# An issue order read from a table instead of planned at build time, in a fused attention and two-MLP kernel on one core

## The chip, the cores and the metric

The kernel runs on one core of a Trainium2 chip. A core has five engines with an instruction queue each: PE (TensorE, the matmuls), DVE (VectorE), ACT (ScalarE), POOL (GpSimd) and SP (SyncE, which here issues every transfer). The engines run side by side and wait for each other through semaphores. The metric is the device time of one execution in microseconds, lower is better.

## The reference, cut to what matters

```python
# attention with decay, 2 batches x 8 heads, 768 positions, 64 wide, in blocks of 64
for b in range(nb):
    intra = einsum('bhic,bhjc->bhij', qb, kb) * Dmask
    intra = einsum('bhij,bhjd->bhid', intra, vb)
    inter = einsum('bhid,bhde->bhie', qb * lam_pow, kv_state)
    out[:, :, sl] = intra + inter
    kv_state = lam_block * kv_state + einsum('bhsd,bhse->bhde', kb * rev_pow, vb)
x = out as 1536 tokens x 512
x = (sigmoid(x @ w_gate) * (x @ w_val)) @ w_out      # 512 -> 1536 -> 512
h = x @ w_in
return elu(h) @ w_out2                               # 512 -> 2048 -> 512
```

All inputs are float32.

## The kernel before, in words

The attention goes over six chunks of 128 positions. For each chunk `scores` multiplies keys with queries (tile `st`, from `tin`) and updates the running state (`st<-nat,kd`), and the loop multiplies the masked scores with the values (`x<-pr,nat`) and the queries with the state (`x<-ql,sn`); `split_chunk` then turns the result into the operands of the MLPs. These attention matmuls are plain float32 and use parts of PE's array (64 or 128 rows, 64 columns); the trace shows them as 64\*64 and 128\*64. The MLPs run in the format of 32 bits rounded for PE (the trace's fp32r), on the whole array, 128\*128: each number is split into a high and a low part, and each product takes three matmuls. They go over hidden columns in groups of 256 (six in the first MLP, eight in the second) and use Strassen-Winograd products of half-size blocks, so that DVE, ACT and POOL have many additions between. Weights come in pieces of 1 MB through one buffer `w64`, are rebuilt into floats in `w32` by `fetch` (one ACT and two DVE instructions for each), and are then summed and split. Results gather in `acc`, and the output leaves in 13 transfers from `o`.

`A0`, `B0` and so on are PSUM banks: the trace names a bank's tile after its first use, so that `warm` in the trace is any tile in bank A0 and `direct` any in B0. In the first microseconds 18 matmuls on a zeroed tile `idle` keep PE running while the first loads land (line 771).

Nothing is issued where it is written. Every call in the body is recorded by `Work.record` (line 167) as an `Op` with an estimated duration; `hazards` (line 207) finds what each operation must stay behind; `issue` (line 408) then makes up the order and emits all operations in it. Within an engine the emitted order is the order of execution. The order before comes from a planner: `run` (line 271) is a list scheduler on a model of the five engines, run forwards and backwards for several settings of `stick` (how long PE keeps to one kind of matmul, since a change of kind costs it time) and of `ahead`; `exchange` (line 385) puts the best stages of several plans together, with the borders set by `mark`. The costs are those of `cost` (line 140): for a transfer 440 ns of the queue, and its bytes at 423 bytes a nanosecond.

Below, operations go by the number that `record` gives them, and PE's operations also by their place in PE's order. One operation of the attention stands for a block of 16 to 32 matmuls.

Of the kernel before, what the change touches and what calls it, by code (L numbers as in the profile page):

```python
# [19 lines left out]
P = 128  # L20
B, H, S, D = 2, 8, 768, 64
# [15 lines left out]
WORDS = 4096  # L37

# [89 lines left out]
class Work:  # L128
# [6 lines left out]
    def __init__(self, nc):  # L135
        self.nc, self.ops, self.block, self.marks = nc, [], None, [0]
        for name in ENGINES:
            setattr(self, name, Engine(self, name))

    def cost(self, op, fn, args, kw):  # L140
# [13 lines left out]
        if fn == "dma_start":  # L154
            return 440, n * P * 4 / 423 if op.eng == "sync" else 2000
# [115 lines left out]
    def run(self, preds, key, backward=False, gate=None, stick=0, thrift=20000):  # L271
        ops = self.ops[::-1] if backward else self.ops
        n = len(ops)
        after, left = [[] for _ in range(n)], [len(p) for p in preds]
        for k, p in enumerate(preds):
            for x in p:
                after[x].append(k)
        ripe, soon = {e: [] for e in ENGINES}, {e: [] for e in ENGINES}
        at, start, end = [max(0.0, g) for g in gate] if gate else [0.0] * n, [0.0] * n, [0.0] * n
        free = dict.fromkeys(ENGINES, 0.0)  # L280
        port = behind = 0.0
        queue = 3500.0
        shape = table = None
        told, pages = 0, {}

        def stall(op, t, keep=False):
            late = 0.0
            here = {}
            for m in range((told + self.FIRST) // self.PAGE, (told + op.words + self.FIRST + self.LEAD) // self.PAGE + 1):
                for mark in (m * self.PAGE - self.FIRST - self.LEAD, m * self.PAGE - self.FIRST):  # L290
                    if m < 2 or not told <= mark < told + op.words:
                        continue
                    now = t + late + op.gap * (mark - told) / op.words
                    if mark == m * self.PAGE - self.FIRST:
                        late += max(0.0, here.get(m, pages.get(m, 0)) - now)
                    else:
                        here[m] = now + (self.SLOW if queue > now + 2000 else self.FAST)
            if keep:
                pages.update(here)
            return late  # L300

        for k in range(n):
            if not left[k]:
                heapq.heappush(soon[ops[k].eng], (at[k], k))
        for _ in range(sum(op.eng is not None for op in ops)):
            t, e = min((free[e] if ripe[e] else max(free[e], soon[e][0][0]), i, e)
                       for i, e in enumerate(ENGINES) if ripe[e] or soon[e])[::2]
            while soon[e] and soon[e][0][0] <= t:
                k = heapq.heappop(soon[e])[1]
                heapq.heappush(ripe[e], (key[k], k))  # L310
            rank, k = heapq.heappop(ripe[e])
            if e == "tensor" and stick and ops[k].shape != shape:
                like = min((x for x in ripe[e] if x[0] < rank + stick and ops[x[1]].shape == shape), default=None)
                if like:
                    ripe[e].remove(like)
                    heapq.heapify(ripe[e])
                    heapq.heappush(ripe[e], (rank, k))
                    k = like[1]
            if e == "tensor" and not backward and thrift and stall(ops[k], t) > 100:
                like = min((x for x in ripe[e] if x[0] < rank + thrift and not stall(ops[x[1]], t)), default=None,  # L320
                           key=lambda x: (ops[x[1]].words, x))
                if like:
                    ripe[e].remove(like)
                    heapq.heapify(ripe[e])
                    heapq.heappush(ripe[e], (rank, k))
                    k = like[1]
            op = ops[k]
            if e == "sync":
                late = 300 if queue < t + 2000 or t < 3000 else 1100
                queue = max(t + 2000, queue) + op.took  # L330
                free[e], end[k] = t + op.gap, queue + late
            elif e == "tensor":
                t += 60 if t > free[e] + 1 else 0
                t += self.SWITCH if op.shape != shape else 0
                shape = op.shape
                late = 0.0
                if not backward:
                    late = stall(op, t, True)
                    told += op.words
                free[e], end[k] = t + late + op.gap, t + late + op.took  # L340
            else:
                if op.table and op.table != table:
                    t, table = t + self.TABLE, op.table
                go = max(t, port, behind if e == "gpsimd" else 0) if op.port else t
                free[e], end[k] = go + op.gap, go + op.took
                if op.port:
                    port = free[e]
                    behind = end[k] + self.HANDOFF["gpsimd"] if e == "vector" else 0
            start[k] = t
            done = [k]  # L350
            while done:
                x = done.pop()
                for s in after[x]:
                    f = ops[s].eng
                    near = e == "tensor" or e == "sync" and (ops[s].prev is op or op.prev is ops[s])
                    ready = free[e] if f == e and x == k and near else end[x] + self.HANDOFF.get(f, 0)
                    at[s] = max(at[s], ready)
                    left[s] -= 1
                    if left[s]:
                        continue  # L360
                    if f is None:
                        start[s] = end[s] = at[s]
                        done.append(s)
                    else:
                        heapq.heappush(soon[f], (at[s], s))
        return start, end

    def mark(self):
        self.marks.append(len(self.ops))

    def clocks(self, plans):
        work = [sum(op.gap for op in self.ops[:m] if op.eng == "tensor") for m in self.marks[1:]]
        clocks = []
        for start, end in plans:
            order = sorted((start[k], op.gap) for k, op in enumerate(self.ops) if op.eng == "tensor")
            at, done, clock = 0, 0.0, [0.0]
            for w in work:
                while done + order[at][1] <= w:
                    done += order[at][1]
                    at += 1  # L380
                clock.append(order[at][0] + w - done)
            clocks.append(clock + [max(end)])
        return clocks

    def exchange(self, preds, plans, tries=8):
        bounds = self.marks + [len(self.ops)]
        best = min(plans, key=lambda x: max(x[1]))
        for i in list(range(len(self.marks))) * 2:
            clocks = self.clocks(plans)
            mine = self.clocks([best])[0]  # L390
            ranked = sorted(range(len(plans)), key=lambda r: clocks[r][i + 1] - clocks[r][i])
            for r in ranked[:tries]:
                gain = mine[i + 1] - mine[i] - clocks[r][i + 1] + clocks[r][i]
                if gain <= 0:
                    break
                key = list(best[0])
                for k in range(bounds[i], bounds[i + 1]):
                    key[k] = plans[r][0][k] - clocks[r][i] + mine[i]
                for k in range(bounds[i + 1], len(self.ops)):
                    key[k] -= gain  # L400
                made = self.run(preds, key)
                plans.append(made)
                if max(made[1]) < max(best[1]):
                    best = made
                    mine = self.clocks([best])[0]
        return best

    def issue(self, tc, rounds=7):
        self.hazards()
        n = len(self.ops)  # L410
        preds = [op.preds for op in self.ops]
        turned = [[] for _ in range(n)]
        for k, p in enumerate(preds):
            for x in p:
                turned[n - 1 - x].append(n - 1 - k)
# [33 lines left out]
def tile_decay_attention_two_mlps(  # L449
# [314 lines left out]
    n = 1  # L764
# [309 lines left out]
    for i in range(1, NG1):  # L1074
# [3 lines left out]
        if i in (2, NG1 - 1):  # L1078
            work.mark()
# [118 lines left out]
```

## Time and profile before

| | us |
|---|---|
| median of 3 runs | 582.1 |
| lowest and highest | 581.39, 582.28 |
| the profiled execution | 581.52 |
| its span, first to last instruction | 579.6 |
| PE busy in the span | 569.1 |
| DVE, ACT, POOL busy | 447.8, 312.6, 317.2 |

The profiled execution took 581.52 us, 1.9 us more than the span that its trace covers, and 0.6 us less than the median. A sum that is made on the span is carried over to the median as a difference. PE is busy for nearly the whole span, and a busy PE is not one at its peak: its matmuls overlap, so what counts is the time from the start of one to the start of the next. The attention takes the first 70 us or so, the first MLP runs to about 320 us, and the second to the end; the weight of one group of columns is in use while the next one is prepared.

### The profile page before, as it was taken

How to read it: one execution, taken by the hardware profiler on the slowest of the kernel's cores; microseconds unless marked ns; L12 is line 12 of the kernel's file. 1: busy time of each engine (PE TensorE's matmuls, PEld its weight loads, DVE VectorE, ACT ScalarE, POOL GpSimd, SP SyncE). 2: the span in 40 equal slices, each digit the busy share in tenths (PEclk: the TensorE clock that was granted, in tenths of full speed). 3: DMA queues.
4: the chain of work that ended last, by engine and by line, in shares of the span. 5: the costliest groups of instructions: out<-in, count | busy, mean ns of one | idle time of the engine just before them, and what ended most of it. 6: DMA issues, size and time to landing. Idle time of an engine off the chain costs nothing.

```text
span 579.6 us, 10208 instructions
## 1 busy us (share of the span) xinstructions
PE 569.1 (98%) x3998; PEld 487.2 (84%) x3998; DVE 447.8 (77%) x771; ACT 312.6 (54%) x612; POOL 317.2 (55%) x273
## 2 busy tenths in 40 slices
PE   7899999999999999999999999999999999999997
PEld 4788898888888888888898888888888888888886
DVE  6877844679999989989978994777676667686484
ACT  4893656445345345444457887764746554735160
POOL 2677678875365555553688865574738180712100
PEclk9999999999999999999999999999999999999999
DMA  8946211221221211210140222232222222200014
GB/s 298 411 168 219 75 74 74 74 74 72 74 73 67 80 47 73 98 55 21 72 146 2 74 73 74 72 144 76 73 74 72 74 74 73 74 0 1 0 37 181
DMA packets 10271, 52.03 MB, mean 90 GB/s; under 512 B 1264, under 2 KB 1520, under 8 KB 5744
## 3 DMA queue, kind: packets, MB, share of 16 engines
q1 hardware_dynamic: 10224, 51.39, 24.4%
q8 instruction: 31, 0.51, 0.3%
q14 instruction: 16, 0.13, 0.1%
HBM read 48.24 MB, written 3.15 MB: 89 GB/s over the span
## 4 chain that ended last, share of the span: by engine, by line
PE 89%; ACT 4%; DVE 3%; DMA 3%; issue 1%; SPq 0%; POOL 0%; ACTq 0%; DVEq 0%
PE xu L182 35%; PE st L182 32%; PE direct L182 10%; PE warm L182 9%; PE x L182 2%; DMA w<-in_w_val 1%; DMA w<-in_w_gate 1%; ACT kd L182 1%; ACT w L182 1%; DVE sig L182 1%; DVE sums L182 1%; DVE gl L182 0%; DVE xu L182 0%; ACT sig L182 0%; ACT x143h L182 0%
## 5 line engine op out<-in xcount | busy, mean ns | idle before, releaser
L182 DVE TENSOR_TENSOR acc<-xu,acc 128x512 f32<-128x512 f32 x144 | 96.8, 684 | 21.7 <-PE xu L182 20.9
L182 POOL TENSOR_TENSOR t<-w 128x256 f32<-128x256 f32 (+1 forms) x80 | 69.3, 887 | 70.2 <-DVE w L182 57.6
L182 PE MATMUL xu<-gl,woh 128*128 128x512 f32 (+1 forms) x274 | 107.2, 391 | 0.1
L182 PE MATMUL xu<-gh,woh 128*128 128x512 f32 (+1 forms) x274 | 106.9, 394 | 0.3 <-DVE xt L182 0.2
L182 PE MATMUL xu<-gh,wol 128*128 128x512 f32 (+1 forms) x274 | 106.5, 389 | 0.0
L182 POOL TENSOR_TENSOR wol<-w,woh 128x512 fp32r<-128x512 f32 x34 | 43.4, 1294 | 67.2 <-ACT woh L182 66.5
L182 POOL TENSOR_TENSOR gl<-sig,gh 128x512 fp32r<-128x512 f32 (+1 forms) x30 | 55.0, 1844 | 40.0 <-ACT gh L182 23.9
L182 POOL TENSOR_TENSOR l<-t,h 128x768 fp32r<-128x768 f32 (+1 forms) x38 | 62.6, 1654 | 13.0 <-ACT h L182 4.9
L182 ACT CAST gh<-sig 128x512 fp32r<-128x512 f32 (+1 forms) x66 | 46.7, 714 | 32.5 <-DVE sig L182 31.6
L182 PEld LDWEIGHTS xu<-gh,woh 128*128 128x128 f32 x274 | 51.4, 188 | 11.3 <-DVE xt L182 0.8
L182 PEld LDWEIGHTS xu<-gh,wol 128*128 128x128 f32 x274 | 51.5, 188 | 10.4
L182 PEld LDWEIGHTS xu<-gl,woh 128*128 128x128 f32 x274 | 51.5, 188 | 10.0 <-DVE gl L182 0.5
L182 ACT ACTIVATE sig<-st 128x512 f32<-128x512 f32 (+1 forms) x52 | 29.2, 566 | 53.4 <-PE st L182 35.5
L182 DVE SCALAR_TENSOR_TENSOR w<-w,w 128x1024 uint32<-128x1024 uint32 (+1 forms) x36 | 54.0, 1503 | 0.3
L182 PE MATMUL st<-x143l,h 128*128 128x512 f32 (+1 forms) x150 | 51.8, 347 | 0.0
L182 PE MATMUL st<-x143h,h 128*128 128x512 f32 (+1 forms) x150 | 51.3, 347 | 0.0
L182 PE MATMUL st<-x143h,l 128*128 128x512 f32 (+1 forms) x150 | 50.7, 347 | 0.0
L182 ACT ACTIVATE w<-w 128x1024 f32<-128x1024 f32 (+1 forms) x36 | 39.3, 1092 | 18.0 <-POOL l L182 10.5
L182 DVE TENSOR_SCALAR w<-w 128x1024 uint32<-128x1024 uint32 (+1 forms) x36 | 32.2, 896 | 18.8 <-ACT w L182 18.6
L182 DVE TENSOR_TENSOR wt<-st,wt 128x512 f32<-128x512 f32 (+1 forms) x57 | 31.5, 556 | 14.2 <-PE st L182 13.9
L182 ACT CAST h<-t 128x768 fp32r<-128x768 f32 (+1 forms) x40 | 29.1, 727 | 13.0 <-POOL t L182 12.8
L182 ACT ACTIVATE sig<-sig 128x256 f32<-128x256 f32 (+1 forms) x68 | 34.2, 510 | 1.3
(190 smaller groups left out, 1495.3 us busy)
## 6 DMA issues: line engine op xcount, KB each, us to landing
w<-in_w_out SPq DMA_DIRECT2D x14, 1024.0 KB, 4.8
w<-in_w_in SPq DMA_DIRECT2D x8, 1024.0 KB, 4.8
nat<-in_att SPq DMA_DIRECT2D x12, 512.0 KB, 9.9
w<-in_w_gate SPq DMA_DIRECT2D x5, 1024.0 KB, 4.8
w<-in_w_val SPq DMA_DIRECT2D x5, 1024.0 KB, 4.8
tin<-in_att SPq DMA_DIRECT2D x6, 512.0 KB, 9.7
tin<-in_att SPq DMA_DIRECT2D x3, 1024.0 KB, 11.4
out_t<-o SPq DMA_DIRECT2D x11, 256.0 KB, 2.0
```

Source lines behind the costliest of these rows:

```text
L182: return [getattr(getattr(self.nc, eng), fn)(*(real(a) for a in args), **{k: real(a) for k, a in kw.items()})]
```

## The change

The planner is taken out (`run`, `mark`, `clocks`, `exchange` and the loop in `issue`), and with it the import of `heapq` and the two calls of `work.mark()`. In its place stands a text constant, `ORDER_TABLE`. `order` decompresses it into one 16-bit step for each recorded operation, sums the steps up to a place for each operation, checks that there are as many places as operations and that no operation stands ahead of one it must follow, and returns the operations in order of place. The emission of the order is the same as before, with the dependencies that it adds between DVE and POOL. The body of the kernel, the tiles, the arithmetic and the transfers are untouched. In `cost` the transfer's two numbers are changed; with the planner gone no order is made from them in the kernel.

```diff
+ORDER_TABLE = (
+    'c-qZa35;FUdH(;i-h0m7-Zsmd@yvL}V{DI&?GcXI8uplqr79_<5+F5Ag<7>y*Qg|IBBG|MKr~$_L`qfBAgZ(h7a=7!1Q)P_19pf_yayZa#>;'
...
+)
...
         if fn == "dma_start":
-            return 440, n * P * 4 / 423 if op.eng == "sync" else 2000
+            return 500, n * P * 4 / 410 if op.eng == "sync" else 2000
...
-    def run(self, preds, key, backward=False, gate=None, stick=0, thrift=20000):
...
-    def issue(self, tc, rounds=7):
+    def order(self):
+        raw = np.frombuffer(zlib.decompress(base64.b85decode("".join(ORDER_TABLE))), np.uint8)
+        steps = np.ascontiguousarray(raw.reshape(2, -1).T).view("<i2")[:, 0].astype(int)
+        places = np.cumsum(steps) + np.arange(len(steps))
+        assert len(places) == len(self.ops), "the table is of another program"
+        assert all(places[p] < places[k] for k, op in enumerate(self.ops) for p in op.preds), "an order against a hazard"
+        return np.argsort(places).tolist()
+
+    def issue(self, tc):
         self.hazards()
-        n = len(self.ops)
...
-        start, end = self.exchange(preds, plans)
-        best = max(end), start
-        order = sorted(range(n), key=lambda k: (best[1][k], k))
+        order = self.order()
         behind = mybir.DependencyInfo(mybir.DependencyClass.Sync, mybir.DependencyReason.DATA)
```

The table can be read without running anything: decompressed, it gives the new order of each engine. Some of both orders, as operation numbers:

| | before | new |
|---|---|---|
| operations of PE, DVE, ACT, POOL, SP | 2961, 771, 609, 269, 71 | the same |
| at the same place in the engine's order | | 153, 82, 67, 66, 71 |
| PE, places 24 to 60 | 135, 2 MLP matmuls, 141, 8, 136, 6, 142, 8, then 160, 161, 286, 162, 163, 287, 292, 165, 228 | 135, 141, 21 MLP matmuls, 142, 136, 3, then 160 to 162, 286, 287, 163, 292, 165, 293 |
| ACT, places 13 to 25 | 74, 76, 62 to 65, 78, 66, 80, 67, 68, 69, 214 | 76, 74, 80, 63, 78, 210, 66, 68, 65, 67, 62, 69, 64 |
| ACT, places of 134 (first sigmoid), 166, 168 | 37, 47, 48 | 47, 49, 51 |
| PE's last 12 places | 4665 to 4670, 4673 to 4678 | the same |

135 and 141 are `st<-tin` of chunk 1, 136 and 142 its `st<-nat,kd`, 286 and 292 `st<-tin` of chunk 2, 287 and 293 its `st<-nat,kd`, 160 to 163 and 165 the `x` of chunk 1, 62 to 69 and 150 to 157 the `kd` of chunks 0 and 1 (ACT), 74, 76 and 166, 168 the casts `x11h` of chunks 0 and 1 (ACT), 210 the cast `h25` of a sum that POOL makes, and 228 on the products of chunk 0 with the first values' weight.

## Rows read from the trace of the kernel before

**Rows 1.** The page: span, busy time by engine, PE and its clock in 40 slices

```profile
span 579.6 us, 10208 instructions
PE 569.1 (98%) x3998; PEld 487.2 (84%) x3998; DVE 447.8 (77%) x771; ACT 312.6 (54%) x612; POOL 317.2 (55%) x273
...
PE   7899999999999999999999999999999999999997
...
PEclk9999999999999999999999999999999999999999
```

**Rows 2.** PE's waits for transfers: engine, tile, releaser: us in total, times, longest us

```profile
PE st L182 <- DMA tin<-in_att: 1.4, 2, 0.9
```

**Rows 3.** Timeline of PE to 23 us: start us, busy us, instruction, [idle before]

```profile
11.74 1.78 PE L182 MATMUL x<-pr,nat 64*64 64x64 f32 x64 [2.13 <-DVE w L182]
...
22.86 0.90 PE L182 MATMUL st<-tin 64*64 64x128 f32 x32 [0.89 <-DMA tin<-in_att]
```

**Rows 4.** Windows of 10 us: busy us (instructions) of PE, PEld, DVE, ACT, POOL

```profile
20.00:30.00 10.00, 8.94 (x206) 8.08 (x207) 9.71 (x17) 9.97 (x29) 7.01 (x6) 1.00 1.03 412
...
170.00:180.00 10.00, 10.00 (x53) 8.59 (x52) 9.93 (x15) 4.25 (x8) 8.05 (x8) 1.00 0.30 107
```

**Rows 5.** Timeline of ACT from 15 to 28 us

```profile
15.72 1.28 ACT L182 ACTIVATE kd<-nat,low 128x128 f32<-128x128 f32 x4 [1.20 <-DMA nat<-in_att]
...
23.54 1.28 ACT L182 ACT_TABLE_LOAD   x1
...
27.82 1.05 ACT L182 CAST x11h<-x 128x512 fp32r<-128x512 f32 x2
```

**Rows 6.** Timeline of PE where its kind of matmul changes

```profile
23.69 1.15 PE L182 MATMUL x<-pr,nat 128*64 128x64 f32 x32
24.67 0.64 PE L182 MATMUL st<-nat,kd 128*64 128x64 f32 x16
...
36.82 0.64 PE L182 MATMUL x<-pr,nat 128*64 128x64 f32 x16
37.38 0.39 PE L182 MATMUL warm<-x11h,l 128*128 128x256 f32 x1
37.61 0.40 PE L182 MATMUL direct<-x11h,h 128*128 128x256 f32 x2
...
51.95 0.28 PE L182 MATMUL direct<-x22l,h 128*128 128x256 f32 x1
52.07 0.28 PE L182 MATMUL direct<-x22h,l 128*128 128x256 f32 x1
52.28 0.69 PE L182 MATMUL st<-nat,kd 128*64 128x64 f32 x16
```

**Rows 7.** Timeline of PE, its larger stops from 23 to 80 us

```profile
28.44 0.51 PE L182 MATMUL direct<-x11h,h 128*128 128x256 f32 x2 [0.17 <-ACT x11h L182]
...
35.17 1.20 PE L182 MATMUL x<-pr,nat 64*64 64x64 f32 x32 [0.41 <-ACT kd L182]
...
71.66 0.35 PE L182 MATMUL warm<-x11h,h 128*128 128x256 f32 x1 [0.50 <-ACT xPh L182]
```

**Rows 8.** Timeline of PE around a short stop in the MLPs

```profile
276.24 0.28 PE L182 MATMUL st<-xPh,l 128*128 128x256 f32 x1
276.49 0.50 PE L182 MATMUL xu<-gh,woh 128*128 128x512 f32 x1
276.82 0.40 PE L182 MATMUL xu<-gl,woh 128*128 128x512 f32 x1
```

**Rows 9.** Timeline of the last microseconds: a result handed over, and its bank used again

```profile
574.56 0.28 PE L182 MATMUL xu<-gh,woh 128*128 128x256 f32 x1
...
574.76 1.14 DVE L182 TENSOR_TENSOR o<-xu,acc 128x512 f32<-128x512 f32 x2 [0.67 <-PE xu L182]
...
575.51 0.39 PE L182 MATMUL xu<-gh,woh 128*128 128x256 f32 x1
```

More of the change, by code (lines that the diff above doesn't have):

```diff
@@ L1 @@
-import heapq
+import base64
 import re
+import zlib
 from contextlib import ExitStack, contextmanager
@@ L135, in __init__ @@
     def __init__(self, nc):
-        self.nc, self.ops, self.block, self.marks = nc, [], None, [0]
+        self.nc, self.ops, self.block = nc, [], None
         for name in ENGINES:
@@ L269, in hazards @@
             op.preds = sorted(before)
-    def run(self, preds, key, backward=False, gate=None, stick=0, thrift=20000):
[L272 to L406, printed above, removed]
@@ L408, in issue @@
-    def issue(self, tc, rounds=7):
-        self.hazards()
-        n = len(self.ops)
[L411 to L415, printed above, removed]
-        best, plans = None, []
-        for stick in (0, 1500, 4000, 10000, 20000):
-            for ahead in (8e3, 20e3):
-                key, gate, least = list(range(n)), None, 1e9
-                for _ in range(rounds):
-                    start, end = self.run(preds, key, gate=gate, stick=stick)
-                    least = min(least, max(end))
-                    plans.append((start, end))
-                    if best is None or max(end) < best[0]:
-                        best = (max(end), start)
-                    _, back = self.run(turned, [-end[n - 1 - k] for k in range(n)], True)
-                    key = [-back[n - 1 - k] for k in range(n)]
-                    gate = ahead and [least + k - ahead for k in key]
-        start, end = self.exchange(preds, plans)
-        best = max(end), start
-        order = sorted(range(n), key=lambda k: (best[1][k], k))
+    def order(self):
[5 more added lines that the diff above has]
+        return np.argsort(places).tolist()
@@ L1077, in tile_decay_attention_two_mlps @@
         last = i + 1 == NG1
-        if i in (2, NG1 - 1):
-            work.mark()
         wG = prep_pair(w_gate, i, nc.gpsimd)
@@ L1111, in tile_decay_attention_two_mlps @@
         last = i + 1 == NG2
-        if i in (2, NG2 - 1):
-            work.mark()
         wH = prep_pair(w_in2, i, nc.gpsimd)
```

46 lines of the change are left out of this document (added).

## The prediction

> **What bounds the kernel now.** I read the page first: the span is 579.6 us and PE is busy 569.1 of them, at full speed of its clock, with thin slices only at the two ends [rows 1]. DVE, at 77%, comes next, and in the middle of the first MLP it is busy 9.93 of 10 us, yet PE runs there without a gap [rows 4]. So the kernel is bound by PE, and the order can change only what PE loses between its matmuls. The work itself stays: the same 3,998 matmuls.
>
> The losses are of three kinds. (1) The start. The first `x` starts only at 11.74 us, when its values have landed, and PE stops again at 22.86 us for the keys and queries of chunk 2, still in flight [rows 3]; twice and 1.4 us together it waits for such a tile [rows 2]. DMA is saturated then: 412 GB/s in the window from 20 us [rows 4]. (2) Changes of kind in the attention. From one 256-column matmul to the next there are 0.12 us (51.95 to 52.07), but 0.21 when an attention block follows (52.07 to 52.28): 0.09 lost. The first MLP matmul behind a block takes 0.23 (37.38 to 37.61) where 0.12 would do: 0.11 lost. And the block of 16 ahead of it takes 0.56 (36.82 to 37.38), where two blocks in a row take 0.98 (23.69 to 24.67), 0.49 each: 0.07 lost [rows 6]. A round trip costs 0.27 us. (3) Stops, where PE waits for another engine. The larger ones before 80 us stand in [rows 7]. Behind 80 us I went through all starts of matmuls against their usual spacing (0.227 us for 512 columns, 0.12 for 256): some 25 stops, 5.4 us together, most of them between 268 and 353 us. One of them shows the price: at 276.24 the next start comes after 0.25 instead of 0.12 us, and the matmul behind the stop takes 0.33 instead of 0.227, so a wait of 0.13 us costs 0.23 [rows 8].
>
> **The change, part by part.** The table decoded is the change; no time comes out of it, only orders. I set them against the order of the trace.
>
> *Transfers.* SP's order is the same in all 71 places, so a load starts earlier or later only where the instruction that frees its buffer moves. The transfer numbers in `cost` are read by no planner any more: 0 us. For the weights of the MLPs nothing was to be had from later landings: PE's only waits with a transfer as their releaser are the two for `tin` [rows 2]. Up to 22.86 us nothing can be gained: the loads in front are the same ten in the same order.
>
> *Up to 22.86 us.* The new order puts one more block of `x` (0.5 us) ahead of operation 286, so less is left when the load lands. But its `kd` come later on ACT: the cast 210 now stands between them, and the last `kd` of chunk 0 is ACT's 26th operation, not the 25th. In the trace the `kd` start at 15.72 [rows 5], and eight of them with two copies end at about 18.7; with the cast (0.7 us) that is 19.4. PE, which now runs 21 matmuls first, comes to 142 at about 18.0, waits for 19.4, and then the masked scores (four DVE instructions of 0.5 us, three of them ahead of the second `x`) hold the `x` until 21.9 and 22.4; 286 starts near 23.3. Half a microsecond less to do, half a microsecond later: 0, between -0.5 and +0.5.
>
> *Changes of kind behind 22.86 us.* Of 40 in the old order the new one keeps 30: four round trips between attention and MLP matmuls fewer (8 entries instead of 12), and two changes between attention shapes. Four times 0.27 are 1.1 us; for the two others, which no row shows alone, I take between 0 and 0.1 each, nearest to the exit's 0.07. Together -1.2 us (-0.8 to -1.4). Nothing can hide this: PE is the bound there.
>
> *ACT from 23 to 31 us.* ACT is busy 9.97 of 10 us in that window [rows 4], so what it does first decides. The new order puts the casts 210 and 87 (0.7 us each) and the second half's `kd` ahead, and the table load with the first sigmoid (1.28 us and 0.5, at 23.54 in the trace [rows 5]) from place 37 to 47, directly ahead of the casts `x11h` of chunk 1. The first of these began at 27.82; item by item I get about 29.1. PE needs them at its places 73 and 75 and has enough other work for all but 0.3 to 0.8 us. +0.5 us (0 to +1.0).
>
> *The stops from 28 to 80 us.* The old order's stops at 28.44, 35.17 and 71.66 [rows 7] cost, counted from start to start with the slow matmul behind them, 0.4, 0.5 and 0.8 us: 1.7. Counted in PE's own work between what they wait for and themselves, the first two get more room, by 1.0 and 2.1 us. The third falls to two matmuls (565 and 558): one gets 2.6 us more room, the other 0.4 less. The first two gained and half of the third are 1.3 us (0 to -1.7).
>
> *The stops behind 80 us.* For each of some 2,650 PE operations I took the chain from the last matmul that it hangs on, through the other engines by their mean durations, and the PE work that the order puts between; the difference is its spare time. The shortest chain is a result taken out of a bank and the bank used again: at the end of the trace a slot ends at 574.56, DVE starts at 574.76, and PE starts at 575.51, 0.95 us in all, where the order had six matmuls (0.72 us) between; it stopped for 0.23 [rows 9]. In the old order 11 operations have under 0.2 us to spare and 65 under 0.5; in the new one 79 and 166. Of the 65, three stopped, for 0.12 to 0.26 us. At that rate 166 give eight, five more, at 0.13 us and up, with 0.1 behind each [rows 8]: about +1.2. Against it, the stops of the old order with long chains (at 311 to 317 us and later) mostly get more room in the new one; I take half a microsecond for that. +0.6 us, between -3 (over half of the 5.4 us gone) and +4.
>
> *The end.* The last 12 matmuls are the same; one matmul of the group before (4654) stands three places later, so its result is handed over 0.7 us later. The stop of 0.23 us [rows 9] changes its place, not its size: 0 (-0.1 to +0.2).
>
> The sum: 0 - 1.2 + 0.5 - 1.3 + 0.6 + 0 = -1.4 us on a span of 579.6, 578.2. The profiled execution took 1.9 us more than its span, and 0.6 less than the median, so the median comes to 582.1 - 1.4 = 580.7 us.
>
> One page speaks for much more room. The Trainium skill, "Perfetto Trace Analysis", section "Identifying the Most-Contended Engine", says that PE's distance to its limit is read from the busy share of the weight loads, not from that of the matmuls. By the 84% here [rows 1] as much as 16% of the span would be open to an order. The spacing of the matmuls, which is at its floor but for the stops counted above, doesn't bear that out, and I give it no chance.
>
> **The rivals.**
>
> *A much better order*: over half of the stops behind 80 us vanish as well, and the time falls by 3.5 us or more, to about 577.5. For it speaks that most old stops get more room; against it, the thinner spare times.
>
> *Gains eaten up*: the changes of kind bring their 1.2 us, and new stops of the same size take them, so that the time stays within 1.2 us of before, say 581.9. That is the case, too, in which the table is just another order of the same worth. For it speaks that the sum is small beside its unknowns.
>
> *Slower by thin spare times.* The place is the MLPs behind 80 us, the mechanism is a bank that is handed back late because DVE, at 9.93 of 10 us, is still at something else [rows 4], the price 0.23 us each [rows 8]. Eleven more stops, one in seven of the 79 thin places, cost 2.5 us, which is more than the 1.2 of the changes of kind; thirteen and no gain at the stops before 80 us give 582.1 + 3.0 - 1.2 + 0.5 = 584.4. From about six extra stops on, the change is no gain. Against it: in the old order none of the nine places with 0 to 0.2 us to spare stopped.
>
> *Slower by ACT's queue in the attention*: the casts of chunk 1 come late for every chunk that follows, and the loads that wait for the freed buffers with them. At 15.72 ACT stood for 1.20 us at a `kd` whose transfer had not landed, with the copies of a finished `x` behind it [rows 5]. This rests on ACT working in order. The Trainium skill, "TensorE: Matmul & The Clock Gate", in its table of the engine's data, says the same: a strict queue on ACT, DVE and POOL, and on PE only weight loads pulled forward. A late item of 1 us in each of three chunks less the 1.2 us and half of the gained stops gives +1.1 us, near 583.3.
>
> **How the numbers follow.** A measurement of this kernel can tell a change of about 0.2%, 1.2 us, from none. A moderate gain, the forecast: 0.37. The much better order: 0.08. Together faster: 0.45. Gains eaten up: 0.31. Thin spare times: 0.17, ACT's queue: 0.07, together slower: 0.24. The bounds of all parts added up would reach from 572 to 588, which would need all of them to err to one side; the range from 577.3 to 584.4 leaves out about 1 in 10 on either side. It takes in the much better order's time and that of the thin spare times; the forecast's own range is 578.6 to 580.9.
>
> **What would show it.** Right: `st<-tin` of chunk 2 starts between 22.8 and 23.4 us; 30 changes of kind behind it; no stop at 35 us; PE reaches the first MLP's second group about 1 to 2 us earlier; a handful more stops of 0.1 to 0.3 us in the MLPs, at accumulations (`xu`) above all. Wrong: a stop of over 0.5 us before 45 us, for `x11h` or `kd`; stops behind 80 us of over 8 us together, or under 3; a load landing later than before.

## The result and the profile after

| | before | after |
|---|---|---|
| median, us | 582.0 | 585.5 |
| lowest and highest, us | 581.39, 582.28 | 584.42, 586.22 |
| the profiled execution, us | 581.52 | 584.42 |
| its span, us | 579.6 | 582.3 |

The change made the kernel slower: the ratio of the times is 1.0059, with a 95% interval from 1.0044 to 1.0074, or 3.5 us. (Five executions of each; the median of before came out as 581.98.) The profiled execution of the new kernel is the lowest of its five, so the traces show 2.7 us of the difference; what the rest is made of no trace shows.

The page after, span, busy time by engine, PE and its clock in 40 slices, against [rows 1]:

```profile
span 582.3 us, 10146 instructions
PE 571.6 (98%) x3998; PEld 483.7 (83%) x3998; DVE 434.5 (75%) x771; ACT 314.4 (54%) x612; POOL 313.5 (54%) x273
...
PE   7799999999999999999999999999999999999997
...
PEclk9999999999999999999999999999999999999999
```

PE is busy 2.5 us longer for the same 3,998 matmuls at the same clock, and the page says no more than that. Where the time goes is found by setting the start of each matmul against the start of the one that has the same amount of PE's own work ahead of it in the other trace (times between two starts are interpolated):

| PE's own work done, us | at, before | at, after | difference |
|---|---|---|---|
| 14 | 21.22 | 21.09 | -0.13 |
| 17 | 25.22 | 24.89 | -0.33 |
| 20 | 28.62 | 29.21 | +0.60 |
| 35 | 44.55 | 44.83 | +0.29 |
| 62 | 73.64 | 72.11 | -1.53 |
| 68 | 80.19 | 78.20 | -1.99 |
| 80 | 92.32 | 90.64 | -1.68 |
| 150 | 162.65 | 162.72 | +0.06 |
| 300 | 314.98 | 316.68 | +1.70 |
| 450 | 468.21 | 469.80 | +1.59 |
| 556.7 (just ahead of the last matmul) | 576.14 | 578.89 | +2.75 |

At 80 us the new order leads by 2.0 us, as forecast. From there to the end it loses 4.7 us, in small pieces. The view of waits, for PE's matmuls from 92 to 576 us (tile, releaser: us in total, times, longest us), first before, then after, hardly shows them:

```profile
PE xu L182 <- DVE xt L182: 0.2, 1, 0.2
```

```profile
PE direct L232 <- DVE wt L232: 0.2, 1, 0.2
PE warm L232 <- ACT wt L232: 0.2, 1, 0.2
PE st L232 <- POOL l L232: 0.2, 1, 0.2
```

The same view of the weight loads (PEld) does. Before, the four largest of 12 lines, which come to 5.7 us in 21 waits:

```profile
PEld st L182 <- DVE sig L182: 1.3, 5, 0.4
PEld xu L182 <- DVE xt L182: 0.8, 2, 0.4
PEld xu L182 <- DVE acc L182: 0.7, 3, 0.3
PEld xu L182 <- DVE gl L182: 0.5, 1, 0.5
```

After, the six largest of 16, which come to 10.7 us in 45 waits:

```profile
PEld xu L232 <- DVE acc L232: 2.0, 11, 0.2
PEld st L232 <- DVE sig L232: 1.8, 8, 0.3
PEld st L232 <- POOL l L232: 1.3, 4, 0.6
PEld direct L232 <- DVE wt L232: 1.1, 3, 0.4
PEld xu L232 <- ACT gh L232: 0.9, 4, 0.3
PEld warm L232 <- ACT wt L232: 0.8, 3, 0.4
```

A weight load stands ahead of its matmul, and it is the load that waits for the matmul's operand. It can be late without its own matmul being late; the matmul behind pays. One such place of the kernel after, PE's matmuls (start, busy):

```profile
161.36 0.28 PE L232 MATMUL warm<-xPl,h 128*128 128x256 f32 x1
161.48 0.50 PE L232 MATMUL xu<-sums,woh 128*128 128x512 f32 x1
161.82 0.40 PE L232 MATMUL xu<-xt,woh 128*128 128x512 f32 x1
162.05 0.39 PE L232 MATMUL xu<-sums,woh 128*128 128x512 f32 x1
```

then their weight loads, and DVE, which frees the bank:

```profile
161.25 0.19 PEld L232 LDWEIGHTS warm<-xPl,h 128*128 128x128 f32 x1
161.47 0.19 PEld L232 LDWEIGHTS xu<-sums,woh 128*128 128x128 f32 x1
161.58 0.19 PEld L232 LDWEIGHTS xu<-xt,woh 128*128 128x128 f32 x1
161.82 0.19 PEld L232 LDWEIGHTS xu<-sums,woh 128*128 128x128 f32 x1
```

```profile
160.74 0.68 DVE L232 TENSOR_TENSOR acc<-xu,acc 128x512 f32<-128x512 f32 x1
```

DVE is done at 161.42 (160.74 + 0.68). The matmul at 161.48 starts on time, 0.12 behind the one before, and no idle time is marked. But its load began only at 161.47, the next load at 161.58, and the next matmul comes 0.34 instead of 0.227 us later. Below, such a place is called a near miss: the operand is there 0.06 to 0.15 us ahead of the matmul that reads it.

Counted behind 92 us over all starts of PE, with a matmul as "waiting" if the last instruction that it depends on ended less than 0.062 us before its start (worked out from the starts and ends in the traces; no view shows it):

| | before | after |
|---|---|---|
| matmuls that wait | 18 | 22 |
| near misses | 19 | 56 |
| lost at the waits and directly behind them, us | 4.31 | 4.25 |
| lost directly behind near misses, us | 0.92 | 3.08 |
| changes from 256 to 512 columns | 139 | 343 |
| lost in steps of up to 0.02 us each, us | 1.89 | 4.22 |
| together, us | 7.1 | 11.5 |

The loss of 4.4 us behind 92 us is 2.2 behind near misses and 2.3 in steps of up to 0.02 us; the waits cost the same in both. The experiments had to find what both come from.

### The profile page after: what moved, and what is told of

It is laid out like the page before. It is cut to its first block, busy times and chain, and to the rows that moved or that the text cites. A ratio compares the mean times of both kernels' runs of the same rounds, so it can differ in the third digit from the quotient of the medians.

```text
span 582.3 us, 10146 instructions
## 1 busy us (share of the span) xinstructions
PE 571.6 (98%) x3998; PEld 483.7 (83%) x3998; DVE 434.5 (75%) x771; ACT 314.4 (54%) x612; POOL 313.5 (54%) x273
## 4 chain that ended last, share of the span: by engine, by line
PE 91%; ACT 3%; DMA 3%; issue 1%; DVE 1%; POOL 0%; SPq 0%; DVEq 0%; ACTq 0%
PE xu L232 37%; PE st L232 33%; PE direct L232 10%; PE warm L232 9%; PE x L232 2%; ACT kd L232 2%; DMA w<-in_w_val 1%; DMA w<-in_w_gate 1%; POOL l L232 0%; ACT w L232 0%; ACT h L232 0%; SPq L232 0%; ACT x11h L232 0%; ACT x143h L232 0%; DVE o L232 0%
## 5 line engine op out<-in xcount | busy, mean ns | idle before, releaser
L232 PE MATMUL xu<-gh,wol 128*128 128x512 f32 (+1 forms) x274 | 105.1, 391 | 0.0
L232 PE MATMUL xu<-gl,woh 128*128 128x512 f32 (+1 forms) x274 | 105.0, 391 | 0.0
L232 PE MATMUL st<-x143h,h 128*128 128x256 f32 (+1 forms) x150 | 50.5, 351 | 0.0
L232 DVE SCALAR_TENSOR_TENSOR w<-w,w 128x1024 uint32<-128x1024 uint32 (+1 forms) x36 | 45.6, 1268 | 0.4
L232 ACT ACTIVATE sig<-st 128x512 f32<-128x512 f32 (+1 forms) x52 | 29.2, 566 | 29.0 <-DVE st L232 15.8
L232 DVE TENSOR_SCALAR w<-w 128x1024 uint32<-128x1024 uint32 (+1 forms) x36 | 28.6, 797 | 13.1 <-ACT w L232 12.6
L232 ACT CAST h<-t 128x512 fp32r<-128x512 f32 (+1 forms) x40 | 29.0, 726 | 16.9 <-POOL t L232 15.8
```

The lines of the kernel that those rows point to most:

```text
L232: return [getattr(getattr(self.nc, eng), fn)(*(real(a) for a in args), **{k: real(a) for k, a in kw.items()})]
```

## Experiments

In the diffs the order is told as operation numbers of PE, since the table itself can't be read; "W us" is an amount of PE's own work. All kernels are the new one with another table, and the body is the same, unless it is said otherwise. Ratios are against the kernel before on the same chip.

### Attention or MLPs: each half with the other order

The first pair cuts at 80 us of PE's work (about 92 us).

```diff
-order = new
+order = new up to W = 80 us, then old        (e1_att_new_mlp_old)
+order = old up to W = 80 us, then new        (e2_att_old_mlp_new)
```

> The new order up to PE's work that the old order has done at 92 us, the old order for all behind it. Theory A (the new order gains in the attention and loses in the MLPs): about 1.7 us under the kernel before, 580.3 (579.5 to 581.0). Theory B (ACT's queue in the attention makes the loss): 584 or more. Nothing is left out of the computation.

> The opposite: the old order to the same point, the new one behind it. Theory A: the MLPs' loss without the attention's gain, 582.0 + 4.5 = 586.5 (585.5 to 587.5). Theory B: 582 (581.5 to 582.7).

Measured: 586.6 us (ratio 1.0075 [1.0057, 1.0094]) and 589.5 us (1.0121 [1.0104, 1.0138]). The first lies where theory B has it (584 or more), the second where neither does. But the totals can't decide here: the two orders have different matmuls behind them at the cut, and the seam makes stops of its own; the first kernel's PE, and its clock in windows of 4 us (the columns are busy us and instructions of PE, PEld, DVE, ACT, POOL, then the granted clock, DMA share, GB/s):

```profile
120.14 0.80 PE L226 MATMUL st<-x11h,h 128*128 128x512 f32 x1 [2.30 <-ACT sig L226]
```

```profile
116.00:120.00 4.00, 1.84 (x14) 1.56 (x12) 3.97 (x6) 0.51 (x1) 3.25 (x3) 1.00 0.00 0
120.00:124.00 4.00, 3.86 (x17) 3.55 (x18) 2.37 (x7) 1.67 (x4) 2.52 (x2) 0.57 0.01 2
```

The totals say nothing, then, but the course behind the seams does: from the work that the kernel before does at 126 us to the end, the kernel with the old MLPs loses 0.2 us against it, the one with the new MLPs 3.0, and the change itself 3.2. So the loss goes with the order in the MLPs.

The cut was then put where only 14 operations of all engines lie on different sides, at 60 us of PE's work (about 71 us).

```diff
-order = new
+order = new up to W = 60 us, then old        (e6_seam70_new_old)
+order = old up to W = 60 us, then new        (e7_seam70_old_new)
```

> The new order up to about 71 us (60 us of PE's own work), where only 14 operations of all engines lie on different sides in the two orders, and the old order behind it. In the traces the new order was 0.6 us ahead there. Theory A (the attention came out as forecast, the loss is made in the MLPs): 582.0 goes to 581.4 (580.8 to 581.9). Theory C (the new attention leaves later work late, ACT's queue above all, and the MLPs pay for it): 584 or more.

> The other way round: the old order up to about 71 us, the new one behind it. Theory A (the loss is made in the MLPs): 585.5 + 0.6 = 586.1 (585.4 to 586.8). Theory C (the loss comes from the new attention): 582.0 to 582.6.

Measured: 583.0 (1.0012 [0.9994, 1.0030]) and 586.6 us (1.0079 [1.0063, 1.0095]). The second agrees with theory A: the old attention in front of the new MLPs is as slow as the change. The first lies between the theories, and its executions spread as those of no other kernel, from 581.1 to 586.9, five of twelve at or below 581.8, where theory A has them. The profiled one, 586.9, shows what comes on top in some:

```profile
59.48 0.44 PE L225 MATMUL x<-ql,sn 64*64 64x128 f32 x5 [2.20 <-issue]
```

```profile
56.00:60.00 4.00, 1.80 (x43) 1.32 (x40) 2.50 (x5) 1.65 (x3) 1.71 (x2) 1.00 0.14 55
60.00:64.00 4.00, 4.00 (x22) 4.00 (x23) 2.64 (x8) 1.88 (x7) 2.52 (x2) 0.57 0.02 4
```

PE stands for 2.20 us at no wait that the profile shows, and behind it the granted clock is 0.57 on average, part of the 4 us at the lower of its two levels. The new attention has this stop in other kernels too, at the same block of matmuls (2.03 us in the first hybrid), while the trace of the change has none there.

What PE waits for can be read from the traces. They hold 16 stops of over 0.2 us that the profile calls "issue", in the twelve traces of the whole kernel, and these stand at two places only, whatever the order: behind 223 of PE's matmuls (in eleven traces, near 17 us) and behind 1,113 (in five, near 58 us), or one less where a record is missing. Each of the 16 ends 1.29 to 1.56 us behind the end of a transfer on the instruction queue (q8 in the profile): behind the first such transfer at the one place, behind the eighth at the other. In e6 the eighth falls in the window from 56.9 to 58.2 us and ends at 57.92; after the change it falls in the one from 54 to 56.9 and ends at 55.49, before PE is there:

```profile
q8 instruction: 1, 0.02, 4.4%
```

```profile
q8 instruction: 1, 0.02, 1.9%
```

So what PE waits for there is its own instructions, as far as traces can tell; no run moved these transfers alone. Why they land later in one kernel than in another is open; from 54 to 56.9 us the loads (q1) had 71.5% of the DMA engines' time in e6 and 25.0% after the change. The rest of e6's excess is 1.9 us between 300 and 400 us of PE's work, most of it one stop of 1.49 us at 368.63, behind a weight load for which ACT had waited 1.76 us.

### The widths of the matmuls

The steps of up to 0.02 us sit on 512-column matmuls behind 256-column ones, and the new order changes width more than twice as often. To see whether the widths alone cost time, the old order got 150 more changes, by exchanging two neighbours at places with at least 0.6 us to spare:

```diff
-1451 1452 1453 1535 1536 1537 1538 1539 1540 1597
+1451 1452 1535 1453 1536 1537 1538 1539 1597 1540
```

(1535 to 1540 have 256 columns, the others 512.)

> The old order, in which 150 pairs of neighbouring matmuls of PE are swapped, one of 512 and one of 256 columns each, at places with at least 0.6 us to spare on both sides; the orders of the other engines are as they were. PE then goes from 256 to 512 columns 304 times instead of 154. Theory A1 (a 512-column matmul is slower for a few places behind a 256-column one, some 14 ns for each change as the two traces have it): 150 times 14 ns, +2.1 us, 584.1 (583.2 to 585). Theory A2 (the loss in the MLPs is only late hand-overs at thin places): no change, 582.0 (581.6 to 582.5).

Measured: 583.95 us (1.0032 [1.0022, 1.0042]), as A1 said. Of the 2.1 us that the trace loses behind 92 us, 1.3 are in the steps of up to 0.02 us, 0.009 for each of 146 changes there; the rest is at five more waits. So 0.0125 us for each change, the price taken for the next expectations, was too much: it had some waits in it.

PE alone was measured with this (attention, MLPs and all else left out, the output is zeros):

```diff
+    runs("s512", [(512, 6, 0)] * 32)
+    runs("s256", [(256, 6, 0)] * 32)
+    for size in (12, 6, 3, 2, 1):
+        runs(f"mix{size}", [(512, size, 0), (256, size, 0)] * (96 // size))
+    runs("two", [(512, 1, 0), (512, 1, 1)] * 96)
```

> PE alone, with all of attention and MLPs left out: stretches of 192 matmuls of 512 columns, of 256 columns, and of both in turns of 12, 6, 3, 2 and 1 (96 of each), and 192 of 512 columns in two banks by turns. Theory A1, if the slower pace lies in PE: a mixed stretch takes longer than half of the two plain ones, by 10 to 20 ns for each change from 256 to 512, so about 0.1 us with turns of 12 and 1 to 2 us with turns of 1. If the pace comes from the other engines' traffic: no difference between the stretches beyond 0.1 us.

Its PE timeline, the two pure runs and the first mixed ones:

```profile
24.41 43.81 PE L60 MATMUL s512n512a<-x,w 128*128 128x512 f32 x192
68.06 23.07 PE L60 MATMUL s256n256a<-x,w 128*128 128x256 f32 x191
90.97 2.91 PE L60 MATMUL mix12n512a<-x,w 128*128 128x512 f32 x12
...
124.41 1.55 PE L60 MATMUL mix6n512a<-x,w 128*128 128x512 f32 x6
125.80 0.88 PE L60 MATMUL mix6n256a<-x,w 128*128 128x256 f32 x6
126.51 1.55 PE L60 MATMUL mix6n512a<-x,w 128*128 128x512 f32 x6
```

192 matmuls of 512 columns take 43.65 us from the first start to the next section's, 0.2274 each (0.2267 once steady; the first takes 0.335 and the next five 0.229 to 0.236), and 191 of 256 columns 22.91 us, 0.1200 each. Six of each would be 2.084 us; from 124.41 to 126.51 they take 2.10. In the five mixes a change to 512 columns costs between 0.002 and 0.016 us net: the 512-column matmuls behind it come 0.228 to 0.236 us apart for about five matmuls, the 256-column one a little early. Two banks in turn cost nothing (43.67 us). The effect lies in PE and is small: turns of 12 cost 0.1 us, as expected, but turns of 1 cost 0.8, where 1 to 2 were.

Then the widths were put together again, in both orders, where nothing depends on it and no spare time falls under 0.45 us; one such place in the new order:

```diff
-1594 1595 1605 1550 1551 1596 1597 1552 1439 1553 1554 1555 1440
+1594 1595 1596 1597 1605 1439 1550 1551 1552 1553 1554 1555 1440
```

> The new order, but behind 75 us PE's neighbouring short runs of 512- and 256-column matmuls are exchanged where nothing depends on it and no spare time falls under 450 ns: 149 changes from 256 to 512 columns instead of 365 (the kernel before has 154). The other engines' orders are the new ones. Theory A (each such change costs PE some 12.5 ns: 1.9 us for 150 in the run with more widths): 216 changes fewer give -2.7 us, and the thin spare times, 109 operations under 0.5 us instead of 160, perhaps -0.3 more: 585.5 goes to 582.6 (582.0 to 583.3). Theory B (the new order loses in the MLPs by late banks and by the other engines' orders, the widths only go with it): within 0.6 us of 585.5.

> The old order with the same exchange: 107 changes from 256 to 512 columns instead of 154, the other engines unchanged. Theory A (12.5 ns for each): -0.6 us, 582.0 goes to 581.4. Theory B: no change, 582.0, or slower where an exchange made something late.

Measured: 583.1 (1.0016 [1.0004, 1.0028]) and 581.8 us (0.9993 [0.9982, 1.0005]). The first lies where theory A had it, the second between A's 581.4 and B's 582.0, too close to tell them apart. The first number was misleading: behind 92 us that kernel gained 1.1 us in steps of up to 0.02 us, but as much at waits and near misses, of which it has 64 instead of 78. Regrouping had moved the thin places apart as well. That called for a run in which the two go against each other.

### Near misses

Here PE's matmuls behind 66 us were exchanged until few of the new order's operands came late or nearly late, by the durations of the trace and the prices seen so far (a wait with what is behind it, and 0.165 us less the spare time behind a near miss). In the first kernel the widths were not looked at; the second starts from the kernel with fewer changes of width and prices those too; the third does the same to the old order.

```diff
-order of PE = new
+order of PE = new, matmuls exchanged for spare time                (e8_new_wide_spares)
+order of PE = e4_new_fewer_widths, exchanged for spare time, width (e9_new_both)
+order of PE = old, exchanged for spare time and width              (e10_old_both)
```

> Seen in the traces so far, behind 92 us: a matmul that waits for another engine, however short, is followed by one that starts 0.10 to 0.115 us late, and one whose operand lands only 0.06 to 0.15 us ahead of its start without a wait is followed by one that starts late by about 0.165 us less that spare time. Waits and near misses of this kind: 17 and 17 before, 14 and 53 after the change. This kernel is the new order with PE's matmuls behind 66 us exchanged, each by a few places, until some 25 of the 67 are left; the widths are not looked at, and there are more changes from 256 to 512 columns, 428 instead of 343 behind 92 us. The other engines keep the new order. Theory S (spare times cost, width is the smaller part): -4.9 us by the durations of the trace and these prices, 585.5 goes to 580.6 (579.6 to 582.5). Theory W (width changes alone are the loss): 85 more at some 8 ns, 586.2.

> The new order with fewer changes of width, 583.1, with its matmuls behind 66 us exchanged further until waits and near misses are some 15 instead of 54, changes of width priced too (241 instead of 132 behind 92 us). Theory S with the width as a smaller part: -5.8 us by the same working, 577.3 (576.5 to 579.5). Theory W: 109 more changes at 8 ns, 584.0.

> The same done to the old order: waits and near misses from 34 to some 20, stops shortened, 193 instead of 139 changes of width behind 92 us. Theory S: -3.4 us by the same working, 582.1 goes to 578.7 (577.9 to 580.5). Theory W: 54 more changes, 582.5. If both this and the kernel before it come out at or below 580, the version with the new attention should be the faster by its lead at 92 us, about 1.5 us.

Measured, with the same count as above, behind 92 us:

| kernel | us | changes of width | waits | near misses | at and behind waits | behind near misses | steps up to 0.02 |
|---|---|---|---|---|---|---|---|
| before | 582.0 | 139 | 18 | 19 | 4.31 | 0.92 | 1.89 |
| after | 585.5 | 343 | 22 | 56 | 4.25 | 3.08 | 4.22 |
| e3, old, more widths | 584.0 | 285 | 23 | 18 | 5.24 | 0.85 | 3.17 |
| e4, new, fewer widths | 583.1 | 132 | 18 | 46 | 3.79 | 2.41 | 3.11 |
| e5, old, fewer widths | 581.8 | 95 | 18 | 18 | 4.20 | 0.93 | 1.72 |
| e8, new, wide spares | 581.1 | 419 | 8 | 22 | 1.92 | 1.15 | 3.92 |
| e9, new, both | 579.4 | 236 | 12 | 11 | 2.90 | 0.52 | 2.18 |
| e10, old, both | 583.0 | 185 | 22 | 15 | 5.00 | 0.62 | 2.18 |

e8 decides between the two theories: with 76 more changes of width than the change it is 4.4 us faster (ratio 0.9979 [0.9968, 0.9990]), where theory W had it slower. DVE, ACT and POOL keep their new orders in it, so these alone don't make the new kernel slow. But of the 4.6 us that its trace saves behind 92 us 2.3 are at waits, where the change had lost no more than the kernel before; 1.9 are behind near misses. It shows that late operands cost more than widths, and not how the change's own loss divides. Its weight loads behind 92 us wait for 2.9 us, in 13 waits, not for 10.7 in 45; the largest lines:

```profile
PEld xu L231 <- DVE acc L231: 0.9, 4, 0.3
PEld st L231 <- DVE sig L231: 0.6, 3, 0.3
PEld xu L231 <- DVE o L231: 0.5, 2, 0.3
```

e9, at 579.4 us (0.9952 [0.9939, 0.9965]), is faster than both kernels of this case, by 2.7 us than the one before. It is 2.1 us above the value that was expected, just inside its bounds.

e10 failed: 583.0 (1.0018 [1.0009, 1.0027]) instead of 578.7. The exchange had counted on waits that vanish, and there are 22 of them instead of 18. One place shows why the working was wrong. DVE in e10:

```profile
145.64 1.55 DVE L227 TENSOR_TENSOR xt<-sig,sums 128x512 fp32r<-128x512 f32 x1
```

and in the kernel before:

```profile
146.34 0.86 DVE L182 TENSOR_TENSOR xt<-sig,sums 128x512 fp32r<-128x512 f32 x1
```

POOL runs a `l<-t,h` of 1.3 us beside both, from 145.34 in e10 and from 145.36 before. In e10 DVE's operation lies beside it for 1.0 us and takes 0.69 us longer than in the other, where they overlap for 0.3. The exchange took each duration from the old trace, as if it were the operation's own; here one depends on what POOL does at the same time. The twelve operations of this kind in the kernel before bear that out: without an overlap they take 0.68 us, with 0.31 us beside a POOL addition 0.87, with 0.92 us 1.47. Not every addition does it: two in e10 lie beside one for 0.70 us and take 0.68. Why the same working held for the new order is open.

### The near miss by itself

Last, PE and DVE alone: 73 times a matmul whose result DVE copies, four (or three) others, the matmul that reads the copy, and 12 more, with copies of 64 to 512 columns, so that the copy ends at different times ahead of its reader.

```diff
+    for between, columns in SWEEP:
+        t = late[count[0] % 4]
+        got = mm("made", x[:, 0], "maker")
+        nc.vector.tensor_copy(out=t[:, :columns], in_=got[:, :columns])
+        fill(between)
+        mm("used", t, "user")
+        fill(12)
```

> PE and DVE alone (attention, MLPs and all else left out, the output is zeros): 73 times the same sequence of 512-column matmuls, 12 of them, one whose result DVE copies to a tile, four (or three) more, and one that reads the tile; the copy's width, 64 to 512 columns, sets how long before its turn the reading matmul finds its operand. Theory S: behind a reader whose operand landed 0.06 to 0.15 us before its start, the next matmul starts late by 0.165 us less that time, though nothing waited; behind one that waited, by 0.105 to 0.115 us; behind one whose operand was there over 0.17 us earlier, not at all. Theory N (near misses in the kernels come from something else that is busy then): no delay behind a reader that did not wait.

Two of the 73, first one whose copy ended at 127.65 (127.01 + 0.64), 0.06 us ahead of its reader, with PE, the weight loads and DVE:

```profile
127.72 0.49 PE L62 MATMUL user<-late,w 128*128 128x512 f32 x1
128.04 0.86 PE L62 MATMUL filler<-x,w 128*128 128x512 f32 x3
```

```profile
127.70 0.19 PEld L62 LDWEIGHTS user<-late,w 128*128 128x128 f32 x1 [0.25 <-DVE late L73]
127.81 1.12 PEld L62 LDWEIGHTS filler<-x,w 128*128 128x128 f32 x5
```

```profile
127.01 0.64 DVE L73 CAST late<-maker 128x464 fp32r<-128x464 f32 x1 [3.56 <-PE maker L62]
```

then one with 0.18 us:

```profile
98.80 0.39 PE L62 MATMUL user<-late,w 128*128 128x512 f32 x1
99.03 0.84 PE L62 MATMUL filler<-x,w 128*128 128x512 f32 x3
```

```profile
98.67 0.19 PEld L62 LDWEIGHTS user<-late,w 128*128 128x128 f32 x1
98.81 0.87 PEld L62 LDWEIGHTS filler<-x,w 128*128 128x128 f32 x4
```

The reader starts on time in both; the matmul behind it comes after 0.327 and after 0.227 us. Over the whole sweep:

| operand there ahead of its reader, us | to the next matmul, us |
|---|---|
| 0.053 to 0.055 (the reader waits, 0 to 0.07 us) | 0.335 to 0.341 |
| 0.063 | 0.325, 0.327 |
| 0.081 | 0.312, 0.313 |
| 0.098 | 0.293 |
| 0.114 | 0.277, 0.279 |
| 0.131 | 0.258, 0.259 |
| 0.149 | 0.250, 0.251 |
| 0.158 to 0.28 | 0.226 to 0.239 |
| over 0.28 | 0.226, 0.227 |

Theory S holds to the hundredth, without anything else running. The chain can be read from the loads: a load starts 0.053 us behind the landing, the next load 0.108 behind it, and that load's matmul 0.23 later; the sum is 0.391, so the next matmul comes 0.391 us less the spare time behind the reader, or 0.227, whichever is more. (That is for readers of 512 columns. Behind a reader of 256 columns that waits, the traces before and after the change have 0.222 to 0.228 us in place of 0.12, the same 0.10 late.)

## Why the prediction was wrong

Predicted were 580.7 us in a range from 577.3 to 584.4; it came to 585.5, outside the range and on the other side.

*Transfers, up to 22.86 us*: right in the sum (-0.13 us at 21.1), not in its items. The `kd` were earlier than worked out (142 starts at 18.50, not behind 19.4), the first `x` of chunk 1 at 20.31 and not 21.9, 286 at 22.68 and not 23.3; instead PE stood 1.02 us at 17.35 in a stop whose releaser the profile calls "issue", the wait for instructions described above. The kernel before has it too, 0.76 us at 17.76, and the prediction's list of losses leaves it out.

*ACT from 23 to 31 us*: right in size, wrong in the operand. Between 24.9 and 29.2 us the new kernel loses 0.9 us, where +0.5 (0 to +1.0) was worked out. I had PE wait for the casts `x11h`; it waits for the sigmoid behind the table load, which holds the bank:

```profile
28.56 0.50 PE L232 MATMUL warm<-x11h,h 128*128 128x256 f32 x2 [1.25 <-ACT sig L232]
```

```profile
26.61 1.28 ACT L232 ACT_TABLE_LOAD   x1
27.91 0.60 ACT L232 ACTIVATE sig<-warm 128x512 f32<-128x512 f32 x1
```

In [rows 5] the table load stands at 23.54; it is 3.1 us later.

*Changes of kind* and *the stops from 28 to 80 us*: right together. The three steps of the attention were to give -1.2 + 0.5 - 1.3 = -2.0 us; at 78.2 us the lead is 1.99, and the stops of [rows 7] are gone. That it fits to 0.01 us is luck: the middle step cost 0.9 and not 0.5, and the other two brought 2.8 and not 2.5, although there is a new stop, for ACT, that no term had:

```profile
40.07 1.10 PE L232 MATMUL x<-ql,sn 64*64 64x128 f32 x32 [0.87 <-ACT low L232]
```

The runs don't tell the two apart.

*The stops behind 80 us*: this is the step that failed. The term was +0.6 us with bounds of -3 and +4; it measured +4.7. The mechanism was named, and is the one rival's: "bank that is handed back late", more places with little to spare. Both the count and the price were taken wrong. The prediction says that in the old order "none of the nine places with 0 to 0.2 us to spare stopped", and takes from that a rate of one stop in 22 of the places under 0.5 us. I had looked for the stop at the thin place itself. It stands one matmul later: of the 11 places under 0.2 us one stopped, but seven have a matmul behind them that is over 0.02 us late. In the new order 34 of the 78 that the trace shows have one, 2.7 us together. Even [rows 8] shows it: the matmul behind the stop takes 0.33 us, and I booked the extra 0.1 as a consequence of the stop; m2 shows that it comes without one. Seven in 11 at 0.066 us each (0.46 us together) would have given 3.3 us for 79 places, 2.8 more than in the old order. With the half microsecond against it that makes +2.3 for the term and +0.3 for the sum: a loss, but a small one. It explains 1.7 of the 4.1 us by which the term was off; the slower pace below is most of the rest.

*The pace*: the other part was not a term at all. "The work itself stays" took 0.227 and 0.12 us for fixed. A 512-column matmul is up to 0.009 us slower for some matmuls behind a change of width, a wait or a near miss. Fitted over nine traces, the steps of up to 0.02 us come to 0.29 us, 0.006 for each change of width and 0.024 for each wait or near miss, to within 0.5 us. By that, 204 more changes cost 1.3 us and 41 more waits and near misses 1.0. So of the 4.4 us lost behind 92 us some 3.1 go back to thin spare times and 1.3 to the widths. That split is worked out from a fit, not measured; that late operands cost more than widths is what e8 measured.

*The weight loads*: the Trainium skill, "Perfetto Trace Analysis", section "Identifying the Most-Contended Engine", has one judge how close PE is to its limit by the busy share of its weight loads, beside the rate of its arithmetic, and not by that of its matmuls. I gave this no chance. Its busy share says little here (84% before, 83% after), but the waits of the same row of instructions show the loss, 5.7 against 10.7 us, where those of the matmuls show 0.2 and 0.6.

*The end*: right; the last stop is 0.26 us, at 577.54 (from 577.05, with 0.227 for the matmul between), where [rows 9] have 0.23.

*The range*: the bounds of all parts added up reach from 575.4 to 587.0, not "from 572 to 588". The measured time lies inside them, although the term that failed lies outside its own.

The rival "thin spare times", at 584.4 and a chance of 0.17, was nearest, though its price was 0.23 us for each of a few new stops, and what came was about 0.06 behind each of some 37 more near misses. The other named sign of a failure, a stop of over 0.5 us before 45 us, came twice, for ACT's sigmoid and at 40.07 and not for `x11h` or `kd`, and was made good by 78 us.

## What to carry to other kernels

Ask for the waits of the weight loads, not only of the matmuls, and look for the cost of a late operand one matmul behind it. In these kernels an order of matmuls wants each operand some 0.16 us before its reader starts (0.39 before the matmul behind a reader of 512 columns), and a search over orders should price that, and, far less, each change of a matmul's width; it should not keep durations fixed for DVE operations that run beside POOL's. A stop that the profile calls "issue" is worth setting against the transfers of the instruction queue. With nothing exchanged but PE's order, two kernels here lie 6 us apart (579.4 and 585.5).

## What the runs showed of the hardware

A wait of PE has a floor: however short it is, the matmul behind it comes 0.10 to 0.115 us late, in every kernel looked at, and an operand that is there 0.08 us ahead of a reader which waits for nothing still costs 0.085 (m2). The Trainium skill, "TensorE: Matmul & The Clock Gate", section "Step-by-step: what each phase is for", says that PE pulls weight loads ahead of running matmuls and that the matmuls stay in order. The trace agrees: in m2 a reader's load starts 0.224 us ahead of its matmul where the operand is early, and that lead shrinks to 0.01 us as the operand nears. That the next load keeps behind the waiting one (0.108 us) is what makes the price.

A 512-column matmul in this format takes 0.2267 us in a steady run (m1), and 0.228 to 0.236 for about five matmuls behind a change from 256 columns, in turns of six the same 16 times over, to the nanosecond. Behind a wait or a near miss the next ones take 0.223 to 0.240 (m2).

PE stops of 2.2 and 2.3 us were followed by a granted clock of 0.57 on average over 4 us (from 60 us in e6, from 120 us in e1), so part of that at the lower of its two levels (1.2 and 2.4 GHz), and such a stop costs more than it lasts: e1 falls back by 4.1 us at its stop of 2.30. PE waits for its instructions at two places of this program, 1.29 to 1.56 us beyond the end of a transfer on the instruction queue, for up to 2.20 us (e6). A DVE operation on two tiles that took 0.86 us took 1.55 where it ran longer beside a POOL addition.
